# One load of a batch's k, issued as three transfers of 80, 35 and 13 rows

## The chip, the core and the metric

The kernel runs on one core of a Trainium2 chip. The metric is the device time of one execution in microseconds (us). Before the change it is 419.84 us, the median of three runs (419.35 to 419.85).

## What is computed

A linear attention over 8 batches of 8 heads (576 rows, head size 64), and behind it a mixing of the 64 lowest frequencies of the sequence, a channel product and a residual:

```python
phi = lambda x: np.where(x > 0, x, np.exp(x) - 1) + 1
kv  = einsum('bhsd,bhse->bhde', phi(k), v);  z = phi(k).sum(over s)
x   = (phi(q) @ kv) / (phi(q) . z + 1e-6)            # -> [8, 576, 512]
X   = rfft(x, over s)[:64]                           # 64 modes
Y   = X * (w_r + i w_i) per mode                     # w_r, w_i: [64, 512, 512] float32
u   = x + irfft(Y);  out = u + relu(u @ w_ch)
```

The two weight arrays are 134 MB of float32; they are read once and turned into bfloat16 by the transfer itself.

## The kernel before

**Stage A** (to about 114 us of the span) is the attention, batch by batch. The whole order of the instructions is fixed by hand: `pin` keeps each engine's instructions as they are written. The loop over the batches `b` (line 440) first calls `load(b + 2)`, so that q, k and v of a batch are fetched two batches ahead into two buffers each (`bufs=2`). After it come the transposes of q (`turn_q`), the sums over k and v (`sum_kv`), the features of the next batch (`features`, which reads k on VectorE), the exponentials of the batch after that (`exps`, line 204, the first reader of a k tile) and the forward transform.

**Loads.** In `load` each of q, k, v of a batch is seen as 128 rows; a row is two runs of 1152 float32. One transfer from GpSimd's queue (line 182) writes them as float16 into a tile of 128 partitions. In the order of GpSimd's queue the load of batch 5's k stands behind that of batch 5's q and ahead of batch 5's v and of one half of weight pair 0. Transfers from this queue take turns on eight semaphores, and a transfer waits for the one that held its semaphore eight transfers earlier.

**Stage B** (to about 387 us) takes the weights, two modes to a pair, 32 pairs. `w_load` (line 109) fetches one pair in two transfers of 64 rows (w_r, then w_i; 1 MB each as written). There are five tiles for the first pairs and then two that alternate, so the transfers of pair p + 2 are issued when the 16 matmuls of pair p (`product`, line 498) have read their tile. `mode_pair` also does other work between the pairs (rows, channel products). The last pair is loaded by `w_load_last` in smaller pieces (line 121), so that little is left to do when its last piece lands. **Stage C** adds the inverse transform of the last modes, the channel product's rest and the residual, and stores the output.

Three other small transfers matter below: the load of the transform's table, `fwd_sb` (line 179, 81 rows of 1024 bytes, from SyncE's queue), and the two `YZ_all<-rows_ahead` (line 1067), each of 12 rows, one from SyncE's queue and one from GpSimd's.

Of the kernel before, what the change touches and what calls it, by code (L numbers as in the profile page):

```python
# [33 lines left out]
def kernel(  # L34
# [10 lines left out]
    nc = tc.nc  # L45
# [52 lines left out]
    pin = tc.keep_in_program_order  # L98
# [66 lines left out]

    qT_all = [q_tile(f"qT{b}") for b in range(B)]
    raw, phi, x16s, xfs = {}, {}, {}, {}

    def load(b):
        for nm, src in (("q", q), ("k", k), ("v", v)):  # L170
            rows_in = src[b].rearrange("h s d -> (h s) d").rearrange(
                "(hp r j) d -> r hp (j d)", r=128, j=2 * NJ
            )
            if (nm, b) == ("q", 0):
                for c in range(2):
                    t = sA.tile([128, 2, NJ * Dh], F32, tag="x16", bufs=2, name=f"q32_{c}")
                    pin(nc.sync.dma_start(out=t, in_=rows_in[:, :, c * NJ * Dh : (c + 1) * NJ * Dh]))
                    raw[nm, b, c] = t
                pin(nc.sync.dma_start(out=fwd_sb[0:FROWS, 0:NJJ, :], in_=fwd_dr.ap()))
                continue  # L180
            t = sA.tile([128, 2, 2 * NJ * Dh], F16, tag=f"{nm}16", bufs=2, name=f"{nm}16_{b}")
            pin(nc.gpsimd.dma_start(out=t, in_=rows_in))
            raw[nm, b] = t

    def heads(nm, b, c):
# [222 lines left out]
    def transform(b, dc):  # L408
# [17 lines left out]
        if dc == NDC - 1:  # L426
# [3 lines left out]
            pin(nc.scalar.mul(out=xv[:, :, 0, :], in_=xf[:, :, 1, :], mul=-SPEC))  # L430

    load(0)
    load(1)
    ones_where(id16, -1, 1, 0)
    make_turns()
# [4 lines left out]
    for b in range(B):  # L440
        if b + 2 < B:
            load(b + 2)
            if b % 2 == 1:
                w_next()
        turn_q(b, 0)
        turn_q(b, 1)
        if b == 0:
            fold_table()
        sum_kv(b)
        if b + 1 < B:  # L450
            for _ in features(b + 1):
                pass
        if b + 2 < B:
            exps(b + 2)
        for jj in range(NJJ + 1):
            form_x(b, jj)
            if b == 0 and jj == 0:
                make_place()
            if b > 1 and jj == 1:
                place_x(b - 2)  # L460
            if b > 0 and jj in (2, 3):
                transform(b - 1, jj - 2)
        if b > 0:
            transform(b - 1, 2)
            transform(b - 1, 3)
# [204 lines left out]
    def x_of(t: int):  # L670
        if t < B * NJJ:
            return x_main[t // NJJ][:, t % NJJ, :]
        i = t - B * NJJ
        return x_tail[i // 2][:, i % 2, :]
# [232 lines left out]
    for b in range(B):  # L907
        pairs += [(b * NJJ, b * NJJ + 1), (b * NJJ + 2, b * NJJ + 3)]
        if b % 4 == 3:
            k = b // 4  # L910
# [222 lines left out]
    def sums_of(n: int, tiles_of):  # L1133
        channels(n, tiles_of)
        add_inverse(n, 1, tiles_of)
        for i in tiles_of:
# [6 lines left out]
            out=x_of(0), in0=accs[0][:, 0], scalar=0.0, in1=x_of(0), op0=ALU.max, op1=ALU.add  # L1143
# [51 lines left out]
```

## Time and profile before

| | us |
|---|---|
| median of three runs | 419.84 |
| the profiled execution, whole | 419.94 |
| its span, from the first to the last instruction | 418.2 |
| TensorE busy in the span | 295.0 (71%) |
| VectorE busy | 240.2 (57%) |
| ScalarE busy | 153.2 (37%) |
| GpSimd busy | 61.3 (15%) |
| batch 5's k issued, landed, first read | 46.05, 57.73, 61.96 |
| last piece of the last weights landed | 387.30 |

Outside the span lie 419.94 - 418.2 = 1.7 us. A transfer is cut into packets, which up to 16 DMA engines move; each of the 16 engines ends its share with a completion write of its own, and the transfer has landed when the last of the 16 has come. The trace holds every packet with its time, but not the number of the engine that moved it.

### The profile page before, as it was taken

To read this page: it belongs to the slowest core of one execution; us is meant where nothing else is said; L and a number is where in the kernel's file an instruction comes from. 1 tells how busy PE (TensorE), PEld (TensorE's weight loads), DVE (VectorE), ACT (ScalarE), POOL (GpSimd) and SP (SyncE) were. 2 spreads that over 40 slices of the span, in tenths; PEclk is the share of its full clock that TensorE was granted. 3 is DMA by queue.
4 is the path that set the end of the run, shared out by engine and by line. 5 is a ranking of instruction groups with operands and counts; after the bars stand their busy time and mean duration, and the time that the engine had idled before them with its cause. 6 is when DMAs were issued, how large, how long until landed. Compare 5 with 4: busy or idle time off the path is not lost.

```text
span 418.2 us, 6982 instructions
## 1 busy us (share of the span) xinstructions
PE 295.0 (71%) x2890; PEld 158.9 (38%) x2890; DVE 240.2 (57%) x533; ACT 153.2 (37%) x226; POOL 61.3 (15%) x110
## 2 busy tenths in 40 slices
PE   0279999999674455444435676978796967998992
PEld 0167777777411222212122232333342422453431
DVE  4779879995437474455536453564454534522794
ACT  4667767954200001000000233334352522331682
POOL 6222222300020111111111111111111111130200
PEclk9999999989755655556665589999897988899997
DMA  8999999999999999999999999999999999998698
GB/s 216 212 212 214 211 219 205 222 215 220 212 215 218 213 221 212 216 217 216 218 216 215 219 212 216 218 215 217 216 215 218 215 215 219 215 210 172 210 401 344
DMA packets 16564, 92.86 MB, mean 222 GB/s; under 512 B 2069, under 2 KB 2790, under 8 KB 12374
## 3 DMA queue, kind: packets, MB, share of 16 engines
q0 software_dynamic: 12656, 81.53, 93.8%
q1 hardware_dynamic: 3878, 10.90, 6.9%
q8 instruction: 22, 0.36, 0.3%
q14 instruction: 8, 0.07, 0.0%
HBM read 163.66 MB, written 9.44 MB: 414 GB/s over the span
## 4 chain that ended last, share of the span: by engine, by line
DMA 55%; PE 25%; DVE 10%; ACT 3%; issue 3%; POOL 3%; ACTq 0%; POOLq 0%
DMA w<-in_moe_w_i_dram 52%; PE P L498 5%; PE kvp L258 5%; DVE x_main L965 4%; DMA k<-in_k_dram 3%; DVE x L294 3%; PE xf L417 2%; PE qTp L238 2%; PE xp L385 2%; POOL w L109 2%; PE num L156 1%; PE zl L485 1%; PE z L858 1%; ACT qT L245 1%; PE xf L422 1%
## 5 line engine op out<-in xcount | busy, mean ns | idle before, releaser
L498 PE MATMUL P<-w,xz 128*32 128x512 bf16 x496 | 49.2, 537 | 71.7 <-DMA w<-in_moe_w_i_dram 69.4
L109 POOL DMA_DIRECT2D w<-in_moe_w_r_dram x31 | 17.2, 553 | 247.9 <-PE P L498 246.2
L515 ACT CAST ys<-P 128x512 f16<-128x512 f32 x15 | 8.8, 586 | 118.1 <-PE P L498 112.3
L498 PEld LDWEIGHTS <-xz 128*32 128x32 bf16 x496 | 12.9, 117 | 93.8 <-DMA w<-in_moe_w_i_dram 77.3
L513 DVE CAST ys<-P 128x512 f16<-128x512 f32 x17 | 11.8, 692 | 58.0 <-PE P L498 58.0
L838 PE MATMUL eps<-wch,xTw 128*128 128x512 f16 x144 | 42.0, 420 | 0.0
L819 DVE TENSOR_TENSOR x_main<-ya,x_main 128x512 f32<-128x512 f32 x32 | 22.0, 689 | 20.5 <-PE ya L815 20.3
L821 ACT CAST x16w<-x_main 128x512 f16<-128x512 f32 x32 | 19.8, 618 | 37.1 <-DVE x_main L819 35.4
L258 PE MATMUL kvp<-vpad,ke 32*128 32x130 f16 x576 | 24.0, 265 | 8.5 <-ACT qT L245 8.5
L846 ACT CAST E<-eps 128x512 f16<-128x512 f32 (+1 forms) x40 | 21.2, 540 | 22.4 <-PE eps L838 22.4
L769 PE MATMUL nw<-kv_diag,qT 128*128 128x130 f16 (+1 forms) x160 | 24.6, 297 | 6.4 <-DVE x_tail L782 3.2
L258 PEld LDWEIGHTS <-ke 32*128 32x128 f16 x576 | 22.2, 117 | 10.0 <-issue 9.6
L508 DVE COPY xz<-xt_c 64x256 bf16<-64x256 bf16 x62 | 22.9, 369 | 2.2 <-PE P L498 1.4
L294 DVE TENSOR_TENSOR x<-num,rd 128x512 f16<-128x512 f32 x32 | 22.1, 691 | 1.1
L238 PE MATMUL qTp<-id,qe 128*128 128x128 f16 x144 | 15.2, 289 | 10.1 <-DVE qe L222 9.6
L769 PEld LDWEIGHTS <-qT 128*128 128x128 f16 (+1 forms) x160 | 14.5, 134 | 19.9 <-issue 11.4
L156 PE MATMUL num<-kv_sb,qT 64*128 64x65 f16 (+1 forms) x320 | 16.3, 219 | 5.7 <-DVE x L294 3.3
L245 ACT COPY qT<-qTp 128x1152 f16<-128x1152 f16 x16 | 19.6, 1293 | 2.0 <-PE qTp L238 1.5
L782 DVE TENSOR_TENSOR x_main<-nw,rd 128x256 f32<-128x256 f32 x32 | 11.2, 415 | 15.8 <-PE nw L769 15.8
L830 DVE COPY xTw<-xTp 128x512 f16<-128x512 f16 x36 | 15.0, 416 | 6.8 <-PE xTp L828 6.8
L838 PEld LDWEIGHTS <-xTw 128*128 128x128 f16 x144 | 13.7, 107 | 11.8 <-issue 4.7
L204 ACT ACTIVATE ke<-k 128x2304 f16<-128x2304 f16 x8 | 16.9, 2112 | 2.6 <-DMA k<-in_k_dram 2.6
(153 smaller groups left out, 525.2 us busy)
## 6 DMA issues: line engine op xcount, KB each, us to landing
w<-in_moe_w_r_dram POOLq DMA_DIRECT2D x31, 1024.0 KB, 12.5
w<-in_moe_w_i_dram POOLq DMA_DIRECT2D x31, 1024.0 KB, 16.8
out_dram<-x_main SPq DMA_DIRECT2D x14, 512.0 KB, 3.5
k<-in_k_dram POOLq DMA_DIRECT2D x8, 576.0 KB, 12.0
v<-in_v_dram POOLq DMA_DIRECT2D x8, 576.0 KB, 12.4
q<-in_q_dram POOLq DMA_DIRECT2D x7, 576.0 KB, 11.7
q<-in_q_dram SPq DMA_DIRECT2D x2, 576.0 KB, 4.4
w<-in_moe_w_r_dram POOLq DMA_DIRECT2D x2, 512.0 KB, 11.5
```

Source lines behind the costliest of these rows:

```text
L109: nc.gpsimd.dma_start(out=w_in[p][half::2], in_=two.rearrange("g (r dc) e -> (g r) dc e", dc=NDW))
L156: mm = nc.tensor.matmul(num[hpo][orow, c0 : c0 + 65], qT[rows, hpp, h2, cols], kv_sb[rows, hpp, h2, :])
L238: nc.tensor.transpose(qT_ps[:, j], phi["q", b][:, c, j].rearrange("p o d -> p (o d)"), id16,)
L245: nc.scalar.copy(out=qT[:, :, c * NJ : (c + 1) * NJ], in_=qT_ps.rearrange("p j x -> p x j"))
L258: nc.tensor.matmul(kv_ps[:, h2, 0:130], phi["k", b][r0 : r0 + 32, j // NJ, j % NJ].rearrange("p o d -> p (o d)"), vp[r0 : r0 + 32, :, j, 0 ...
L294: nc.vector.tensor_tensor(out=dst.rearrange("p (o c d) -> p o c d", o=2, c=4), in0=nv[:, :, :, 0:64], in1=rden.unsqueeze(3).broadcast_to([ ...
L498: nc.tensor.matmul(P[c : c + n, :], x, w[:, dc, :], start=(dc < NDC), stop=(dc >= n_dc - NDC), tile_position=(0, c), skip_group_check=True,)
L508: pin(nc.vector.tensor_copy(out=xz[p % 2][HALVES[h], :, h, :], in_=src))
L769: nc.tensor.matmul(num[c][orow, h2 * 130 : h2 * 130 + 130], qT[:, c, h2, rows_of(jj, BASE[b % 2])], kv_diag[:, b, c, h2].rearrange("p o n ...
L819: pin(nc.vector.tensor_tensor(out=x, in0=acc, in1=x, op=ALU.add))
L838: nc.tensor.matmul(e_ps, xT[:, c, :], wch16[:, c, :], start=(c == 0), stop=(c == NDC - 1))
L846: pin(nc.scalar.copy(out=dst, in_=e_ps[:, cols]))
```

## The change

Batch 5's k, one transfer of 128 rows before, is issued as three transfers of 80, 35 and 13 rows, one behind the other, on the same queue and into the same tile. All other loads are as they were.

```diff
     raw, phi, x16s, xfs = {}, {}, {}, {}
+    SHARES = {("k", 5): (80, 35, 13)}
...
             t = sA.tile([128, 2, 2 * NJ * Dh], F16, tag=f"{nm}16", bufs=2, name=f"{nm}16_{b}")
-            pin(nc.gpsimd.dma_start(out=t, in_=rows_in))
+            r0 = 0
+            for n in SHARES.get((nm, b), (128,)):
+                pin(nc.gpsimd.dma_start(out=t[r0 : r0 + n], in_=rows_in[r0 : r0 + n]))
+                r0 += n
             raw[nm, b] = t
```

## The prediction

> **What bounds the kernel now.** I read the page's DMA part first, then the chain that ended last in order of time, then GpSimd's and ScalarE's timelines around the load, and last the packet records.
>
> ```profile
> DMA  8999999999999999999999999999999999998698
> ...
> q0 software_dynamic: 12656, 81.53, 93.8%
> ...
> q8 instruction: 22, 0.36, 0.3%
> ```
>
> The 16 DMA engines are busy from the start to about 387 us, nearly all of it with GpSimd's queue (q0). So what counts is not when one transfer ends but how much each engine has to move. The chain in order of time says the same:
>
> ```profile
> 330.42 17.59 DMA w<-in_moe_w_i_dram
> 348.06 1.08 PE P L498 x16
> ...
> 370.20 2.16 POOL w L121 x4
> 372.36 13.64 DMA w<-in_moe_w_i_dram
> 389.65 1.02 PE acc L892 x4
> ```
>
> In stage B each stretch is "weights land, 16 matmuls, the next load is issued, weights land". Half of those 17.6 us a load stands behind the load before it: while the matmuls run the engines have the other pair in their queues. The PE waits agree:
>
> ```profile
> PE P L498 <- DMA w<-in_moe_w_i_dram: 69.4, 23, 5.7
> ```
>
> **One engine sets the end.** From the packet records I followed each engine by its completion writes, whose distances stay the same to about 1 ns from transfer to transfer (whole loads of q, k, v are 2.787 us apart on an engine, halves of weight pairs 4.853 us). What breaks the step is mostly the 22 instruction packets (q8; 0.36 MB / 22 = 16 KB each): each leaves one engine 1.07 to 1.13 us late, and they go round eight engines. Nothing takes that back, as the queue of a late engine doesn't run dry. At the last weights the 16 engines stand behind the earliest by, in us:
>
> ```
> 3.65 3.48 3.40 3.28 3.22 2.86 2.76 2.66 2.50 | 0.96 0.76 0.60 0.52 0.23 0.19 0.00
> ```
>
> Nine are late, seven early. Landing is the last one's: the last piece came to the first engine at 383.66 us and to the last at 387.30, and the end follows 387.30. So the change in time is: the lateness of the latest engine with the new shares, less 3.65.
>
> **What the change does outside the DMA engines: nothing that reaches the end.**
>
> ```profile
> 46.05 0.71 POOL L182 DMA_DIRECT2D k<-in_k_dram  x1 [1.42 <-ACT kv_sb L270]
> 47.63 0.72 POOL L182 DMA_DIRECT2D v<-in_v_dram  x1 [0.86 <-DVE rd L291]
> 48.34 0.56 POOL L109 DMA_DIRECT2D w<-in_moe_w_i_dram  x1
> 55.79 0.71 POOL L182 DMA_DIRECT2D q<-in_q_dram  x1 [6.89 <-DVE qe L222]
> ```
>
> Two more issues of at most 0.71 us put the third end at 46.05 + 3 x 0.71 = 48.18 instead of 46.76. Batch 5's v is issued 0.55 us later, the weights' half behind it too, and batch 6's q not at all, as it waits for VectorE until 55.79. The engines don't notice: at 48 us the load of batch 5's q is still queued, landing at 54.1, so there are 6 us of cover; without it the price would be 1.4 us. The third piece and the loads behind it wait for semaphores of transfers that landed by 37.6 (batch 3's v), 42.7 and 45.5; all later loads keep their partners, since both have moved by two. The compute side has room as well:
>
> ```profile
> 59.92 2.13 ACT L204 ACTIVATE qe<-q 128x2304 f16<-128x2304 f16 x1
> 61.96 2.11 ACT L204 ACTIVATE ke<-k 128x2304 f16<-128x2304 f16 x1
> ```
>
> The second is batch 5's k, which landed at 57.73, 4.2 us earlier. Batch 6's k (landed 70.27, read at 73.35) has 3.1 us. If the latest engine runs 1.1 us later, both still hold.
>
> **What it does to the engines: the shares.** With 128 rows each engine moves 8 rows, 16 packets; 2.787 / 8 = 0.348 us a row. How are 80, 35 and 13 rows shared? The trace has three shapes that aren't 128 or 64 rows. The table's 81 rows were moved as nine packets on each of nine engines. The two loads of 12 rows used twelve engines each, the four last ones of 4 rows four. That is each time the largest number up to 16 that divides the rows: 80 rows go to 16 engines (5 each), 35 to seven (5 each), 13 to thirteen (1 each). Where do they begin? The 12-row loads from the two queues used the same twelve engines: twelve completion writes of one queue follow those of the other by 326 ns, eleven exactly and the twelfth with its record missing. So I take 35 rows to begin where the 81 rows began. If the 13 go on behind the 35, four engines move 5 + 5 + 1 = 11 rows, three 10, nine 6. If they begin at the first engine again, seven move 11, six 6 and three 5.
>
> [...]
>
> Prices: three rows more +1.04 us, two more +0.70, two fewer -0.70. Each transfer also has a fixed part, 2.787 us less 16 x 0.173 (packet to packet) = 0.02 us; two more cost 0.04 on each engine. An engine without data writes fillers (the 12-row load: about 12 ns each); ten would be 0.12 us, on relieved engines only.
>
> **Who gets the rows?** The nine engines with a table share are slower by nine small packets at 5.4 to 7.6 us, so they can be told from the rest. Followed to the end they are 3.65, 3.40, 3.28, 2.76 and the early 0.96, 0.76, 0.23, 0.19, 0.00; five of the late ones lie outside. (Between 71 and 77 us several engines were held up at once, and there the following is least sure.) Seven of these nine get the 35 rows, so at least two of the four late ones are loaded. If the latest gets three rows (4 places in 9, or 7 in 9 if the 13 begin again), the end moves by 1.04 + 0.04 = +1.08 us. If it gets two, by +0.74, or +0.83 if 3.40 gets three. If it is spared, from +0.36 (2.76 and 3.28 loaded with two) to +0.83. The bounds for any placing are -0.53 (all nine late ones relieved, with fillers) and +1.08.
>
> I forecast the first: 419.84 + 1.08 = **420.9 us** (the profiled execution of 419.94 would be 421.0). A measurement of this kernel tells about 0.2%, 0.84 us, from no change.
>
> **Rivals.**
> - *The latest engine gets two rows or is spared (chance 0.23):* +0.36 to +0.83, 420.2 to 420.7. For it: two or five of nine places. Against it: the others loaded are only 0.25 and 0.37 us earlier.
> - *Even dealing (0.12):* 35 rows as 3 each on eleven engines and 2 on a twelfth, 13 as 1 each. Eleven engines then have 9 rows, +0.35 + 0.04 = +0.39, 420.2. 12 and 4 rows on GpSimd's queue fit this too; against it are the 81 rows, which would have been 6 on each of 14 engines, though from the other queue. [...]
> - *Faster (0.10):* the seven loaded engines are the seven early ones. Seven and nine are just the sizes of the two groups. Then the latest ends 0.70 - 0.04 - 0.12 to 0.70 - 0.04 earlier, about 419.2 to 419.3; the early ones rise to at most 0.96 + 1.08, under 3.65 - 0.66 = 2.99, so the gain holds whole. It decides from the point where none of the engines above 2.3 is loaded (2.3 + 0.70 = 3.0). Against it: four of the late ones carried table rows and the shares seem to start at the same place. A start that moves from one execution to the next would allow it. [...]
> - *Few engines (0.03):* the 35 rows fall to one engine; 32 rows more are +11 us, if it is late, 430.
> - *No change (0.02):* the shares are evened out later, if late engines run dry. In the trace only engines early by then were held up (at 71 us).
>
> **How the numbers follow.** The forecast's case has 0.50. Within it the time is 420.9. The cases from 420.2 to 420.9 hold 0.85; with the scatter of the runs (0.25 us down, as much up) and the unknown start, the range is 419.6 to 421.2, which leaves out the gain and the few-engines case. Slower by over 0.2%: 0.50 + 0.03, 0.53. The gain is priced at 0.13 to 0.16%, near the bound, and what its price leaves out may carry it over: I give 0.07 of it to faster and 0.03 to within. Within 0.2%: 0.23 + 0.12 + 0.02 + 0.03 = 0.40. Faster: 0.07.
>
> **What would show it.** Right: in the packet records the completion writes of the weights after 60 us stand further apart, the last piece's first and last by about 4.7 us or more instead of 3.64, and 35-row and 13-row completions on the empty engines come at once. Batch 6's q is issued at about 55.8 as before, and `PE P L498 <- DMA` grows by no more than a microsecond. Wrong: the last landing spread under 3.65 (the late ones were relieved), all 16 engines taking a share of the 35 rows, or a later q, k or v issue that moves stage A.

## The result and the profile after

The changed kernel takes 420.35 us, median of 22 runs (419.91 to 420.85); the kernel before took 419.42 on the same chip (22 runs, 419.22 to 420.3). The ratio is 1.002, 95% interval 1.0014 to 1.0027: +0.59 to +1.13 us. The profiled execution took 420.01 us with a span of 418.3, only 0.07 more than that of before; why is told with the run `again`.

The page's DMA part after the change (slices; queue: packets, MB, share):

```profile
DMA  8999999999999999999999999999999999998698
...
q0 software_dynamic: 12784, 81.54, 93.7%
...
q8 instruction: 22, 0.36, 0.3%
```

The load of the engines is unchanged, and so are the bytes to 0.01 MB. Queue q0 has 128 packets more. 32 are the completion writes of two more transfers (2 x 16; each transfer of this queue has 16 in the packet records). The other 96 are four-byte fillers of engines without data, and they tell the shares exactly: 35 rows on seven engines leave nine without 5 rows, 10 packets each; 13 rows leave three without 2 packets; 9 x 10 + 3 x 2 = 96. Dealt evenly, it would be 4 x 6 + 2 + 3 x 2 = 32. The packet records have the 96: nine runs of ten from 53.95 us on and three runs of two, at 56.03, 56.09 and 56.30 us. The three engines with two are among the seven that have none of the ten, so the 13 rows begin behind the 35.

The chain in order of time, at the places shown before:

```profile
331.02 16.89 DMA w<-in_moe_w_i_dram
347.95 1.08 PE P L502 x16
...
370.38 2.70 POOL w L121 x5
373.08 13.72 DMA w<-in_moe_w_i_dram
...
389.80 1.02 PE acc L896 x4
```

Same chain, same bound: the weights' landing. `PE acc` starts at 389.80 instead of 389.65. PE's waits for it have grown by 1.3 us over 23 waits:

```profile
PE P L502 <- DMA w<-in_moe_w_i_dram: 70.7, 23, 5.8
```

GpSimd's issues (start, duration, instruction, idle before it):

```profile
46.05 1.88 POOL L185 DMA_DIRECT2D k<-in_k_dram  x3 [1.47 <-ACT kv_sb L274]
47.93 0.74 POOL L185 DMA_DIRECT2D v<-in_v_dram  x1
48.67 0.57 POOL L109 DMA_DIRECT2D w<-in_moe_w_i_dram  x1
53.71 0.72 POOL L185 DMA_DIRECT2D q<-in_q_dram  x1 [4.46 <-ACT qT L249]
```

The three pieces take 1.88 us, v is issued 0.30 us later and the weights' half 0.33. Batch 6's q comes 2.1 us earlier, so nothing on GpSimd cost time. The split alone does not decide that: in the kernels below it comes at 53.7 to 53.9 or at 55.6 to 55.8, and kernels with uneven shares are found in both groups. In this execution ScalarE reads k at 57.69, 0.11 us after it landed at 57.58; the 4.2 us of room seen before were used up by an attention stage that ran ahead.

By the packet records the last piece of the weights came to the first engine at 383.28 us and to the last at 387.45 (before: 383.66 and 387.30).

### The profile page after: what moved, and what is told of

The parts are those of the page before. It is cut to its first block, busy times and chain, and to the rows that moved or that the text cites. A ratio compares the mean times of both kernels' runs of the same rounds, so it can differ in the third digit from the quotient of the medians.

```text
span 418.3 us, 6985 instructions
## 1 busy us (share of the span) xinstructions
PE 291.3 (70%) x2890; PEld 155.6 (37%) x2890; DVE 240.1 (57%) x533; ACT 152.9 (37%) x226; POOL 63.3 (15%) x112
## 3 DMA queue, kind: packets, MB, share of 16 engines
q0 software_dynamic: 12784, 81.54, 93.7%
## 4 chain that ended last, share of the span: by engine, by line
DMA 59%; PE 20%; DVE 9%; ACT 4%; issue 4%; POOL 3%; ACTq 0%; POOLq 0%
DMA w<-in_moe_w_i_dram 52%; DMA k<-in_k_dram 7%; PE P L502 5%; DVE x_main L969 4%; PE kvp L262 3%; PE xp L389 2%; DVE x L298 2%; ACT qT L249 2%; POOL w L109 2%; PE xf L421 1%; PE zl L489 1%; PE z L862 1%; PE num L156 1%; PE acc L896 1%; PE qTp L242 1%
## 5 line engine op out<-in xcount | busy, mean ns | idle before, releaser
L262 PE MATMUL kvp<-vpad,ke 32*128 32x130 f16 x576 | 22.3, 249 | 8.4 <-ACT qT L249 8.4
L262 PEld LDWEIGHTS <-ke 32*128 32x128 f16 x576 | 20.4, 109 | 9.8 <-issue 8.9
L242 PE MATMUL qTp<-id,qe 128*128 128x128 f16 x144 | 13.0, 262 | 13.0 <-DVE qe L226 9.6
L109 POOL DMA_DIRECT2D w<-in_moe_w_i_dram x31 | 17.6, 569 | 5.8 <-DMA q<-in_q_dram 2.2
```

The source lines that it names most:

```text
L109: nc.gpsimd.dma_start(out=w_in[p][half::2], in_=two.rearrange("g (r dc) e -> (g r) dc e", dc=NDW))
L262: nc.tensor.matmul(kv_ps[:, h2, 0:130], phi["k", b][r0 : r0 + 32, j // NJ, j % NJ].rearrange("p o d -> p (o d)"), vp[r0 : r0 + 32, :, j, 0 ...
```

## The experiments

Each run's difference is against the kernel before on the same chip. The edits are shown against the changed kernel, whose `SHARES` line they replace; `marks` and `marks2` are shown against the kernel before. "Position" is an engine's place in the round, counted from where the 35 rows begin.

**Shares or number of transfers: `even`, `more`, `order2`, and the changed kernel `again`.**

```diff
-    SHARES = {("k", 5): (80, 35, 13)}
+    SHARES = {("k", 5): (112, 7, 9)}     # even
+    SHARES = {("k", 5): (64, 49, 15)}    # more
+    SHARES = {("k", 5): (80, 13, 35)}    # order2
```

> Batch 5's k as three transfers of 112, 7 and 9 rows. By the rule that the rows are shared over the largest number of engines up to 16 that divides them, the engines move 7 + 1 rows each (seven of them by the second piece, nine by the third), 8 as before. Theory of the shares (the change costs what it adds on the late engines): 0.0 to +0.15 us against the kernel before, and a last landing as spread as before, about 3.6 us give or take where the instruction packets fall. Theory of the splitting (two more issues, completions and fillers cost by themselves) and theory of the place (what stands behind this load is late): as much as the change, +0.6 to +1.1 us.

> 64, 49 and 15 rows: 4 rows on each engine, 7 more on seven, 1 more on fifteen: 12 or 11 rows on seven engines, 5 on nine. Theory of the shares: the late ones of the seven get one or two rows more than in the change (10), 0.35 to 0.70 us, so +1.3 to +1.8 us against before, if the pieces begin at the same engine in every execution; with a start that moves, anything from -0.9 to +1.8 with a wide scatter. Theories of the splitting and of the place: +0.6 to +1.1 us, as the change.

> The same three pieces with the last two exchanged: 80, 13, 35 rows. If each piece goes on at the engine behind the last one of the piece before, the 35 rows fall to the last three engines and the first four: 11 rows on four engines, 10 on three others, 6 on nine, among them the two late engines that have 10 rows in the changed kernel. The empty engines' fillers are then 3 x 2 + 9 x 10 = 96 as in the change. Theory of the shares: other engines become the last ones; +0.2 to +0.9 us, less than the change if the three last engines are early ones. If pieces always begin at the first engine: seven engines with 11 rows, the two late ones with one more row than in the change, +0.9 to +1.5 us. Theories of the splitting and of the place: no different from the change, +0.6 to +1.1 us.

> The changed kernel again, for the same chip as the others. All theories: +0.6 to +1.1 us. Theory of the shares: 7 engines moved 10 or 11 rows of batch 5's k and 9 moved 6; which of the eight engines with instruction packets gets a third one before the end differs between executions, so the spread of the last landing is 4.1 to 4.8 us; it was 4.17 in the first profile.

The kernel before took 419.47 us on this chip (33 runs). `even` 419.72, ratio 1.0001 (0.9992 to 1.001); `order2` 420.25, 1.0017 (1.0008 to 1.0026); `again` 420.47, 1.0018 (1.0009 to 1.0027); `more` 420.92, 1.0032 (1.0023 to 1.0041). The q0 lines of the pages of `even`, `more` and `order2`:

```profile
q0 software_dynamic: 12720, 81.54, 93.8%
```
```profile
q0 software_dynamic: 12816, 81.54, 93.6%
```
```profile
q0 software_dynamic: 12784, 81.54, 93.8%
```

Less 12656 and 32 completions that is 32, 128 and 96 fillers: 9 x 2 + 7 x 2 (8 rows for every engine), 9 x 14 + 1 x 2 (49 rows as 7 x 7), and 96 again. Three transfers with even shares cost nothing that can be measured (-0.3 to +0.4 us); the price comes with the uneven shares, and the most uneven split costs most. `even` is the run that settles the main question.

In `order2` the engines with rows are partly others: in the packet records the first two hit by instruction packets get 10 rows, while four engines keep their 11. So the start goes on from piece to piece, as in the first of the prediction's two cases.

`again` also explains the pair of profiles. The durations of the 16 KB packets name the engines: in the same order in every execution they are, but for single longer ones, 974, 962, 893, 893, 949, 945, 935 and 974 ns. I call these engines e0 to e7. But the sequence does not begin at the same one: with e0 in the profiles of before, `order2`, `again` (and `four` and `late` below), with e4 in that of the changed kernel, `even`, `more` (and in the other five below). In the first kind e0 to e4 have their third packet before the weights end, in the second e4 to e7 and e0. The last landings, by kind:

| begins at | kernel: last piece landed, us |
|---|---|
| e0 | before 387.30, `order2` 387.67, `again` 387.78 |
| e4 | `even` 387.23, changed 387.45, `more` 387.95 |

The pair before/after was of two kinds, and its 0.07 us is no measure of the change. Within the first kind `again` lands 0.48 us after before.

The profile of `even`, 420.35 us, is its slowest run, and something else sets its end. The chain in order of time:

```profile
347.80 1.93 PE P L502 x16
...
370.74 0.98 PE P L502 x16
...
376.46 2.59 PE zl L489 x12
...
390.12 1.02 PE acc L896 x4
```

The 16 matmuls at 347.80 us take 1.93 us where before and the changed kernel have 1.08, the last weights are issued from 372.03 us on (before: 370.20), and from 347.80 us on TensorE's own work is the chain. `PE acc` starts 2.89 us behind the last landing, in before 2.35. The landings of the last piece stand 1.92 us apart, where about 3.6 were expected. So `even`'s 387.23 is no measure for its kind, and the claim that even shares cost nothing rests on the eleven timed runs.

**Place: the same split on batch 3's k, `k3`.**

```diff
+    SHARES = {("k", 3): (80, 35, 13)}
```

> The same split (80, 35, 13) on batch 3's k in place of batch 5's, some 20 us earlier. If the rows that each engine gets are all that counts, the place is of no matter: the 35 and 13 rows begin at the same engine, the same seven engines get two or three rows more and nothing takes it back in 330 us, so +0.6 to +1.1 us over the kernel before, as with batch 5 (+0.93), and 96 more packets that an engine without data writes. If the price came from batch 5's place (the order of the landings there, a wait of a later load), or if early lateness is made good while the attention runs, the time is within 0.3 us of before.

420.08 us against 419.65, ratio 1.0012 (1.0003 to 1.0021), +0.13 to +0.88 us; q0 has 12784 packets again. The median (+0.4) lies under the forecast, the interval reaches well into it. A place 23 us earlier (22.64 us in place of 46.05) does not remove the price; that it is the same size is not shown.

**Which engine is where: `marks` and `marks2`.**

```diff
+    marks = const.tile([17, 77], F16, name="marks")
+    mark_src = q[0, 0][0:306].rearrange("(p j) d -> p (j d)", p=17)
...
+        if b == 5:
+            c0 = 0
+            for n, w in [(17, 1)] + [(17, w) for w in range(3, 11)] + [(4, 1), (17, 11), (17, 12)]:
+                pin(nc.gpsimd.dma_start(out=marks[0:n, c0 : c0 + w], in_=mark_src[0:n, 0:w]))
+                c0 += w
```

> Twelve tiny transfers behind the loads of batch 7, of 17 rows each (one of 4), from 2 to 24 bytes a row, into a scratch tile that nothing reads; the rest is as before. If rows go to the largest number up to 16 that divides them, from a start that goes on from transfer to transfer, each 17-row one is moved by a single engine, and the next by the next one, so each size of packet tells where in the order an engine stands: of positions 0 to 3 three are early engines and one a late one, of 4 to 6 one early, 7 and 8 early. The time should be that of before plus 12 x 0.02 = 0.24 us and some queueing at 70 to 80 us. If the start does not go on, all the small packets come on one engine; if rows are dealt evenly, they come on 16.

426.38 us in its one run, and the rule failed for these shapes. In the packet records every 17-row load has two packets on each of eight engines and one on a ninth; the fillers agree, 15 for each such load (7 x 2 + 1). In the seven that follow each other directly it is always the same nine engines, in the same order 32 ns behind the load before. So these loads, 17 rows of one run each, went out evenly from a fixed place, while 35 and 13 rows of two runs each went to seven and thirteen engines after the change. Why they differ was not shown. The 6.7 us are a dry queue: with the eight semaphores taken, seven of them by tiny transfers, GpSimd waited 4.38 us from 81.9 us on, and from 86 to 90 us the engines were nearly idle.

```diff
+    marks = const.tile([64, 2, 10], F16, name="marks")
+    MARKS = {
+        2: [(2, 3), (2, 4), (2, 5), (2, 6)],
+        3: [(2, 7), (2, 8), (2, 9), (2, 10)],
+        4: [(3, 1), (2, 3), (2, 4), (2, 5)],
+        5: [(2, 6), (2, 7), (2, 8)],
+    }
...
+        src = k[0].rearrange("h s d -> (h s) d").rearrange("(hp r j) d -> r hp (j d)", r=128, j=2 * NJ)
+        for i, (n, w) in enumerate(MARKS.get(b, ())):
+            p0 = 16 * (b - 2) + 4 * i
+            pin(nc.gpsimd.dma_start(out=marks[p0 : p0 + n, :, 0:w], in_=src[0:n, :, 0:w]))
```

> Fifteen tiny transfers of 2 rows (one of 3) behind the loads of batches 4 to 7, each row two runs as in the loads of k, into a scratch tile that nothing reads; the rest is as before. If these are shared like 35 and 13 rows, the first goes to positions 0 and 1 of the round, the next to 2 and 3, and so on, and after the one of 3 rows to 3 and 4, 5 and 6, 7 and 8: each engine's position can be read. Expected: one late and three early engines at 0 to 3, e2, e3 and one early at 4 to 6, early ones at 7 and 8, e4 to e7 at 9 to 12, and e0, e1 and one early at 13 to 15. If 2 rows always go to the same two engines (as 17 rows of one run went to the same nine), all but the first pairs stay without data.

420.75 us in its one run, against 420.41 in one of the kernel before. With two runs a row, as in the loads of k, each load of 2 rows went to two engines and the next one to the next two; 28 fillers for each of the fourteen loads of 2 rows and 26 for the one of 3 (418 in all) say the same of the shares. By matching the start of each small packet with each engine's lateness (a load of 2 rows starts at two engines whose lateness fits it to some 15 ns) the round is

```
position  0 1 2 | 3  | 4     | 5  6  | 7 8   | 9  10-12     13 14 | 15
engine    early | qA | early | e2 e3 | early | e4 e5-e7 any e0 e1 | early
```

qA is late by the small 8 KB instruction packets (0.53 us each) and none of 16 KB. So 35 rows from position 0, then 13, load e2 and e3 with 10 rows, qA and three early engines with 11, and relieve e0, e1, e4 to e7 and three early ones to 6. The packet records of the changed kernel agree: the two engines that take e2's and e3's instruction packets fall behind by 10 rows, qA and three early ones by 11. In `order2` e0 and e1 get the 10 rows: by the lateness before, e1 ends at 3.28 + 0.74 = 4.02, +0.37, and its last piece landed 0.37 us after that of before. In `more` positions 0 to 5 have 12 rows, 6 has 11: e2, at 3.40, rises by 1.39 + 0.04 to 4.83, +1.18 over 3.65, and +0.96 to +1.72 was measured.

**Dose: `two` and `four`.**

```diff
+    SHARES = {("k", b): (80, 35, 13) for b in (3, 5)}          # two
+    SHARES = {("k", b): (80, 35, 13) for b in (2, 3, 4, 5)}    # four
```

> The split (80, 35, 13) on k of the batches 2, 3, 4 and 5 instead of 5 alone; each of them moves the start of the round by 35 + 13 (that is 48, three times round), so the same engines are loaded each time. If the latest engine gets three rows more each time, as forecast for one, +4 x 1.08 = +4.3 us over before. If the latest one (3.65) gets two rows each time, and the latest that gets three is the one at 2.66, the end is the larger of 3.65 + 4 x 0.74 = 6.6 and 2.66 + 4 x 1.08 = 7.0, so +3.0 to +3.4 us. If late engines are relieved when their queues run dry, less than four times 0.93, with engines held up in the trace. Fillers: 4 x 96.

> The split on k of the batches 3 and 5. Three rows for the latest: +2.16 us. Two rows: the larger of 3.65 + 1.48 and 2.66 + 2.16, +1.5 us. Fillers: 2 x 96.

`four` 420.1 us against 419.68, ratio 1.001 (1.0001 to 1.0019): +0.04 to +0.80. `two` 420.55, 1.003 (1.0013 to 1.0047), five runs. Both expectations were wrong in their premise. With a start that moves by the 48 rows, and so loads the same engines each time, `four` would have lost 3.0 us or more. In the trace after the change the 13 rows begin behind the seven engines of the 35; so the start is taken to move by the engines used, 7 + 13 = 20, which is 4 past a full round, and the four splits to begin at positions 0, 4, 8 and 12. Summed over them, positions 3, 7, 11 and 15 get 29 rows and all others 33 where 32 would be even: e3 gets one row more, 0.35 us, and eight more transfers cost 8 x 0.02. That is +0.5, in the middle of the measured interval. After two splits e3 has 10 + 11 = 21 rows, five more, +1.7 to +1.8; the interval (+0.55 to +1.97) holds it, but the median is +0.87. Four times as many splits cost no more than one, by this reckoning because their unevenness cancels. The premise's failure tells more than its success would have.

**The same pieces, early or late engines: `early` and `late`.**

```diff
+    skip_sb = const.tile([16, 2, 2], F16, name="skip_sb")
...
+    SHARES = {("k", 4): (4, 72, 4, 48), ("k", 5): (36, 68, 24)}
+    SKIP = 15    # early; 9 in late
...
+            if (nm, b) == ("k", 4):
+                pin(nc.gpsimd.dma_start(out=skip_sb[0:SKIP, :, 0:1], in_=rows_in[0:SKIP, :, 0:1]))
```

> k of batch 4 in pieces of 4, 72, 4 and 48 rows, k of batch 5 in 36, 68 and 24, and ahead of them a load of 15 rows of 4 bytes into a scratch tile, which only moves the start of the round to position 15. By the shares (4 rows on four engines, 72 on twelve, 48 on sixteen, 36 and 24 on twelve, 68 on four with 17 each) positions 15, 0, 1 and 2, all four early engines, get 22 rows in place of 16, the twelve others 14. By the records of before: the latest engine is relieved by two rows, 3.65 - 0.70 = 2.95, the early ones end at most at 0.96 + 6 x 0.348 = 3.05, and six more transfers cost 6 x 0.02 to 6 x 0.04. So -0.6 to -0.3 us against before, if only the engines' sums count. If a transfer's fixed part is larger than 0.1 us, or if the 17 rows that land late hold up the attention, no gain or a loss. Fillers (4-byte packets): 1 x 2 for the load of 15 rows, 12 x 2 each for the pieces of 4, 4 x 12, 4 x 6 and 4 x 4 for those of 72, 36 and 24, 12 x 34 for that of 68, 546 in all.

> The same pieces, only the scratch load has 9 rows in place of 15, so the same shares begin at position 9: the 22 rows fall on positions 9 to 12, e4 to e7 or three of them and e0, all late ones, the 14 on the others. Then e4 (3.22) or whichever is latest of them rises by 6 x 0.348 = 2.09: +1.5 to +2.1 us against before, plus the six transfers' 0.1 to 0.2, and 2.0 to 2.7 us over the version that begins at 15. If only the number and shape of the transfers count, both take the same time.

`early` 419.45 us, ratio 1.0 (0.9991 to 1.0009); `late` 421.92, 1.0058 (1.0045 to 1.007), both against 419.55. The pages' q0 lines, `early` first:

```profile
q0 software_dynamic: 13328, 81.54, 94.0%
```
```profile
q0 software_dynamic: 13328, 81.54, 93.7%
```

Same packets in both: 672 over before, which is 6 x 16 completions, 30 of the scratch load's data and the 546 fillers expected (in `late` 18 and 558). Their chains at the last weights, `early` first:

```profile
372.67 13.45 DMA w<-in_moe_w_i_dram
...
389.15 1.02 PE acc L900 x4
```
```profile
375.02 13.28 DMA w<-in_moe_w_i_dram
...
391.35 1.02 PE acc L900 x4
```

Equal transfers, equal shapes, and 2.2 us between these starts (profiles of the two kinds, so good to some tenths), 2.47 between the medians: but for six rows of the scratch load, only which engines carry the rows differs. The loss of `late`, +1.9 to +2.9 us, lies at and above the upper end of what was worked out (+1.6 to +2.3). The gain of `early` did not show: expected -0.6 to -0.3, the interval is -0.4 to +0.4. Its last piece landed at 386.80 us, but no undisturbed profile of even shares that begins at e4 stands beside it, and the medians (-0.10) can't tell a gain. No version was found that beats the kernel before.

## Why the prediction was right, and which step was wrong

The time came out at +0.93 us (0.59 to 1.13) against a forecast of +1.08, and on the side, slower, that had the highest chance. That it came so near is luck: the forecast's sum used a term that the latest engine did not get, and the two profiles of one kind differ by 0.48 at the last landing.

- **Bound, and nothing outside the engines:** right. The chain is the same and the q0 share too (93.8 and 93.7%); GpSimd's issues moved by 0.3 us. `even`, with the same three pieces, is not measurably slower. The stated cover of 4.2 us ahead of ScalarE's read was a property of one execution: it was 0.11 in the next, and ScalarE's waits for loads of k came to 4.0 us there in place of 2.6.
- **Shares of 11, 10 and 6 from where the table began, the first of its two cases:** right; the fillers show the sizes and that the 13 rows go on behind the 35, `order2` and `marks2` the start. The rival of even dealing (0.12) falls with the 96 fillers, the few-engines rival too. That this start holds from execution to execution, which the prediction left open, is so in the traces that were followed. What does move is where the instruction packets begin.
- **Price of a row, 0.348 us:** right. In the packet records after the change the engines with 11 rows fell 1.687 us behind those with 6, those with 10 rows 1.336; five and four rows are 1.74 and 1.39, less some 0.06 that the relieved ones spent on fillers. The fillers' starts stand 6 ns apart; the prediction's 12 ns was twice too large.
- **"If the latest gets three rows": this is the step that failed.** In an execution that begins at e0, as that of before does, the latest engine, e3 at 3.65, is at position 6 and gets two. The term of the sum was 0.70 + 0.04 = +0.74, which the prediction priced as the second case, not 1.04 + 0.04. The measured interval holds both; the traces decide. In `again`, which begins at e0 too, the last three landings are those of qA, e2 and e3, at 387.45, 387.62 and 387.78 us. What misled was the list of late engines with table rows. It had four (3.65, 3.40, 3.28, 2.76). There are three, 3.65 (e3), 3.40 (e2) and 2.66 (qA): 3.28 and 2.76 are e1 and another of the eight, outside. The following had swapped engines where a 16 KB and an 8 KB packet fell into one transfer, at 37.7 us and between 81 and 84, not between 71 and 77 us where the prediction doubted it. Of the three only qA gets three rows, and 2.66 + 1.08 = 3.74 stays under 3.65 + 0.74 = 4.39. In an execution that begins at e4 the other half of the same rival holds: the latest engine is spared. There qA is last, in the changed kernel's profile at 387.45 us, 0.85 behind the next. At a load near the end it completes at 372.37 us and e4 at 371.15; without the split qA would be 1.08 earlier and e4 0.60 later, so e4 would be last and the split would cost about 0.6 us (an estimate from these records).
- **The faster rival** stood on seven loaded engines being the early ones. Four of them are early, three late.
- **What would show it:** half right. The fillers were as said, the issues nearly, and PE's waits grew by 1.3 us where a microsecond at most was named. The spread of the last piece, forecast at 4.7 us or more, was 4.17, and 3.57 in `again`, under the 3.65 that was to mean a relieved late engine, although that kernel is slower (ratio 1.0018); in `even` it was 1.92. The first completion moves too: in the trace after the change the earliest engine, which landed first at 363.30 us, landed its next share 5.40 us later in place of 4.85, its first packet there having taken 1.77 us in place of 1.23. Others landed first then, at 368.54 us, 5.24 us behind the first of the load before, and from there to the last piece the spread was 4.15 to 4.17. How far this goes in `again` and `even` was not shown. The spread of the last piece is no measure of the latest engine; its last landing is, within one kind of execution and where the chain runs through that landing.

What stays open: which of the two kinds each timed run was, as only profiled ones show it, and so how the difference of the medians (0.93) divides over them. One pair of the first kind says +0.48 at the last landing, the estimate for the second about 0.6; both are under the 0.93. The profiled execution of before, 419.94 us, lies 0.52 above the median of its 22 runs, and that of the changed kernel, 420.01, 0.34 under its own, so the lateness of 3.65 need not be that of a typical run.

## What to carry to other kernels

Where the DMA engines are the bound, a transfer's number of rows is a decision about engines: pieces whose shares add up evenly (112, 7 and 9 rows here) cost nothing that was measured (-0.3 to +0.4 us), while pieces of 80, 35 and 13 rows put 11 rows of a 128-row load on some engines and 6 on others, and the end waited for the last engine, +0.93 us. Work the shares out piece by piece, here with a start that goes on from piece to piece, and prove them by the four-byte packets that the queue's line of the page gains (128 here, 96 of them fillers): loads of 17 rows of one run each were shared otherwise. Before comparing two profiles at a fraction of a microsecond, see whether they are of the same kind and whether the same chain ends both; otherwise rest on many timed runs.

## What the hardware showed that was not expected

- A 16 KB instruction packet takes 0.89 to 0.98 us and leaves one of eight engines 1.07 to 1.13 us late; in the trace of before the spread of the landings grew from 1.38 us (the load landing at 81.4 us) to 3.64 at the last piece. These packets go round in a fixed order, but begin at one of two engines from execution to execution (at e0 in five of the thirteen profiles, at e4 in eight), so which engine is latest at the end changes with no change of the program.
- Loads of 17 rows with one run a row were dealt evenly from a fixed place (two rows on each of eight engines, one on a ninth, in `marks`); loads of 2, 13 and 35 rows with two runs a row went to two, thirteen and seven engines, from a start that goes on.
- Lateness among the engines did not even out by itself: in `late`, rows put on the wrong four engines at 36 to 49 us cost 2.4 us at 420 (421.92 against 419.55).
